# A spectral MLP on one core: the inverse transform as plain fp32 matmuls, and a weight conversion whose last addition is done by a DMA

## Chip, cores and metric

The kernel runs on one core of a Trainium2 chip. The metric is the device time of one execution in microseconds (us). Before the change it is 1207.77 us, the median of 3 runs (1206.66 to 1209.07).

## What is computed

Two batches of 3008 x 256 go through a Fourier layer, and the 6016 resulting tokens through two gated MLPs. Everything is fp32 on the host side; the MLP weights are float64 in memory.

```python
X = np.fft.rfft(x, axis=1)
Yr = Xr @ w_r - Xi @ w_i + b_r
Yi = Xr @ w_i + Xi @ w_r + b_i
# soft threshold at 0.01 of Yr and Yi
y = np.fft.irfft(Yr + 1j * Yi, n=3008, axis=1)
h = y @ w_in1;  y = (h * sigmoid(1.702 * h)) @ w_out1     # 256 -> 2048 -> 256
h = y @ w_in2;  y = (h * sigmoid(h)) @ w_out2
```

## The kernel before

The program has four stages, one after the other on TensorE (PE).

**Forward** (`fold`, `fwd_mm`): sums and differences of the inputs, then matmuls with cosine and sine matrices in plain fp32. One plain fp32 product is two MATMUL instructions in the trace (line 342).

**Mid** (`mid_mm`, `mid_post`, `mid_fold`): twelve units (b, p, j), each the complex product with w_r and w_i, the soft threshold on ACT and DVE, and folds `f` of sum and difference (line 502, four of 256 columns for each unit).

**Inverse** (`inv_mm`, `inv_post`, `inv_out`): sixteen units (q, b, t). Before it, `fsplit` splits each folded tile `f` into a high part `fh` (an ACT cast to fp32r, line 99) and a low part `fl` (a subtraction, line 100), 24 times. The matrices lie in memory as high and low parts too, and `product` adds up three fp32r matmuls for each product (line 345): high by high, high by low, low by high. The pool `m` has four buffers; each takes the two parts of one matrix, so four of the eight matrices are loaded ahead and four during the inverse, by DMAs that POOL issues (line 125). `inv_post` copies (ACT, line 586) or adds (DVE, lines 607 and 608) the result, and `inv_out` writes the four combinations to `yt` (lines 625 and 629), each of the two halves `mm` apart.

**MLP** (`group`, `out_mm`): two layers l, six blocks i of 1024 tokens (the last of 896), eight groups p in a block. A group has 21 matmuls into `x` (line 737) and 24 out of the gated `g` into `o` (line 709), of 512 columns in fp32r; the 24 lag by one group. The low part of `g` is a subtraction on POOL or DVE (line 747). `y1` and `y3`, `y2` are summed on DVE at lines 758, 782 and 779.

Beside these stages the float64 weights are converted, a pair at a time. `cv_load` loads a pair, `cv_bits` rebuilds an fp32 value from the bits with one ACT and five DVE instructions (lines 163 to 172), as two parts `a` and `c`; `settle` adds them (line 225, on POOL or DVE); `window` then places the pair (`place_in`, `place_out`: high and low parts, ACT casts and POOL subtractions). One such step is a tick. A pair that has no room yet is spilled to DRAM (line 228) and fetched again later (line 256). `WEIGHTS` sets the order and whether a pair is kept; `CFG` holds the steps at which ticks are made (`tf` forward, `tm` mid, `ti` inverse, `kb` and `kr` the groups of the first and of the later blocks of layer 0), and which engine does each copy of an operation (`V` DVE, `P` POOL). Before the change the out-pairs 0 to 4 of layer 0 are spilled in the mid stage and fetched in the groups p = 0 to 4 of the first block, and the pool `wib` for in-pairs 4 to 7 opens after the first group, when the pool `fs` of the `fh` tiles is closed. In layer 0's later blocks the ticks convert layer 1's weights, all spilled.

Inside a region named in `CFG` with `all`, every engine keeps the order of the program text; elsewhere a scheduler orders the engines that are not named. `hook(h)` in `group` puts the ticks' parts between a group's matmuls: `window` at 1 or 3, loading at 4, `settle` at 6.

Of the kernel before, what the change touches and what calls it, by code (L numbers as in the profile page):

```python
# [56 lines left out]
def spectral_mlp_kernel(ctx, tc, xin, mfwd, minv, wc, bias, w_in1, w_out1, w_in2, w_out2, outT):  # L57
# [419 lines left out]
    def mid_post(i, ps):  # L477
# [35 lines left out]
    fs = {}  # L513
    fsu = [(q, b, p, j) for q in range(2) for b in range(B) for p in range(2) for j in range(NJ)]
    n_fs = [0]

    def fsplit(k):
        for _ in range(k):
            if n_fs[0] < len(fsu):
                u = fsu[n_fs[0]]  # L520
                f = ft.pop(u)
                hi = fs_p.tile([P, 2 * D], F32R, tag="fh", name="fh")
                lo = slot(0, F32R, "fl")
                split(hi, lo, f, lo_eng=E('fsl', n_fs[0]))
                fs[u] = (hi, lo)
                n_fs[0] += 1
# [25 lines left out]
    def inv_mm(q, b, t):  # L552
# [61 lines left out]
    def inv_out():  # L614
        q, b, ac, rt = ydone.pop(0)
        for mm in range(2):
            col = b * S + (0 if q == 0 else HALF)
            for k in range(4):
                e = E('ivf', (b * 2 + mm) * 4 + k)
                op = e.tensor_sub if k in (0, 3) else e.tensor_add  # L620
                x = ac if k < 2 else rt
                u, v = (row(x, mm, t, 378) for t in range(2))
                if q == 0 and k == 1:
                    y = yt[:, mm, col : col + 376].rearrange("p (g c) -> p g c", g=2)
                    op(y, *(z.rearrange("p (g c) -> p g c", g=2)[:, :, :188] for z in (u, v)))
                    col += 376
                    continue
                for i0, i1 in ((0, 188), (189, 376)) if q == 0 and k == 3 else ((0, 377 if (q, k) == (0, 0) else 376),):
# [346 lines left out]
def _matrices():
    fwd = np.zeros((2, 2, 2, P, NJ * 380), np.float32)
    inv = np.zeros((2, 2, 2, P, MW), np.float32)
    for kind, q, p, cs in np.ndindex(2, 2, 2, 2):
# [13 lines left out]
        else:  # L992
            inv[p, q, cs, :, : 2 * nb * w] = np.stack(_hilo(m), 1).reshape(P, -1)
# [37 lines left out]
```

## Time and profile before

| what | value |
|---|---|
| median of 3 runs | 1207.77 us |
| the profiled execution | 1207.06 us |
| its span, first to last instruction | 1204.9 us |
| busy time PE / ACT / DVE / POOL | 1172.0 / 751.8 / 669.5 / 524.5 us |
| share of PE in the chain that ended last | 76% |
| mean granted TensorE clock | 0.994 |
| moved by DMA | 54.44 MB |

Busy time is the time in which an engine has an instruction under way. The chain that ended last is followed back from the last instruction, at each step to what released it. The granted clock is a share of full speed, 2.4 GHz.

### The profile page before, as it was taken

Reading aid. Unit: us, or ns where it says so; the run is one execution under the profiler, and the core shown is the slowest. Engines: PE = TensorE matmul, PEld = TensorE weight load, DVE = VectorE, ACT = ScalarE, POOL = GpSimd, SP = SyncE. Lnnn points to the kernel's source line nnn. Section 1 sums busy time; section 2 is a strip of 40 time slices with the busy share of each in tenths; the row PEclk is TensorE's granted clock in tenths of the full one; section 3 lists DMA queues with packets and bytes.
Section 4 is the critical chain, followed back from the end, with each engine's and each line's share of the span. In section 5 each row is a group of like instructions: output and inputs, shape, how many; then the busy total and the mean of one; then the engine's idle time right before and its main releaser. Section 6 shows DMA issues by size and latency. Waiting matters only on the chain.

```text
span 1204.9 us, 14433 instructions
## 1 busy us (share of the span) xinstructions
PE 1172.0 (97%) x5044; PEld 936.6 (78%) x5044; DVE 669.5 (56%) x1001; ACT 751.8 (62%) x1422; POOL 524.5 (44%) x429
## 2 busy tenths in 40 slices
PE   7999989799999999999999999999999999999998
PEld 4744489577887887887888978878888888888897
DVE  7868999777557556557465372352442533523422
ACT  2533433577767667667667776676676766766765
POOL 2443343564445444444455755433333333333333
PEclk9999999899999999999999999999999999999999
DMA  7542122021011010110110100000000000000000
GB/s 276 186 151 87 44 88 77 27 70 36 27 43 37 27 52 27 45 53 27 36 50 21 54 27 27 1 36 1 1 35 1 1 35 1 35 1 1 35 1 31
DMA packets 27274, 54.44 MB, mean 45 GB/s; under 512 B 2369, under 2 KB 11585, under 8 KB 26434
## 3 DMA queue, kind: packets, MB, share of 16 engines
q1 hardware_dynamic: 26018, 45.03, 11.1%
q0 software_dynamic: 1184, 8.50, 2.0%
q8 instruction: 39, 0.64, 0.2%
q14 instruction: 33, 0.27, 0.1%
HBM read 41.85 MB, written 11.67 MB: 44 GB/s over the span
## 4 chain that ended last, share of the span: by engine, by line
PE 76%; DVE 10%; ACT 8%; issue 4%; DMA 1%; POOL 0%; SPq 0%; DVEq 0%; ACTq 0%; POOLq 0%
PE o L709 33%; PE x L737 30%; PE psm L470 7%; PE psf L342 4%; ACT yt L740 3%; PE psi L345 2%; ACT g L742 2%; DVE yt L758 1%; DMA raw<-in_x 1%; DVE yt L779 1%; ACT yt L756 1%; DVE x L660 1%; DVE yt L629 1%; ACT x L657 1%; DVE cv_a L170 1%
## 5 line engine op out<-in xcount | busy, mean ns | idle before, releaser
L747 POOL TENSOR_TENSOR g<-yt,g 128x512 fp32r<-128x512 f32 (+1 forms) x282 | 366.9, 1314 | 516.0 <-PE x L737 355.6
L709 PE MATMUL o<-g,wo 128*128 128x512 f32 (+1 forms) x2304 | 562.1, 386 | 4.0 <-POOL wo L100 4.0
L737 PE MATMUL x<-x,wi 128*128 128x512 f32 (+1 forms) x2016 | 505.3, 389 | 12.1 <-DVE yt L758 4.2
L709 PEld LDWEIGHTS o<-g,wo 128*128 128x128 f32 x2304 | 432.7, 188 | 87.5 <-POOL wo L100 5.7
L737 PEld LDWEIGHTS x<-x,wi 128*128 128x128 f32 x2016 | 377.1, 189 | 95.5 <-DVE yt L779 6.3
L740 ACT ACTIVATE yt<-yt 128x512 f32<-128x512 f32 (+1 forms) x288 | 179.2, 622 | 267.1 <-DVE yt L779 216.4
L742 ACT CAST g<-yt 128x512 fp32r<-128x512 f32 (+1 forms) x384 | 234.2, 612 | 11.8
L779 DVE TENSOR_TENSOR yt<-yt,x 128x512 f32<-128x512 f32 (+1 forms) x96 | 64.7, 674 | 213.3 <-PE x L737 212.9
L758 DVE TENSOR_TENSOR yt<-yt,x 128x512 f32<-128x512 f32 (+1 forms) x96 | 64.8, 675 | 163.2 <-ACT yt L756 160.6
L747 DVE TENSOR_TENSOR g<-yt,g 128x512 fp32r<-128x512 f32 (+1 forms) x102 | 71.2, 698 | 76.4 <-ACT g L742 75.5
L470 PE MATMUL psm<-wc_s,xt 128*128 128x512 f32 x192 | 84.5, 592 | 0.0
L470 PEld LDWEIGHTS psm<-wc_s,xt 128*128 128x128 f32 x192 | 36.5, 190 | 43.3 <-issue 41.1
L342 PE MATMUL psf<-m,xf 128*128 128x376 f32 (+2 forms) x208 | 59.2, 447 | 7.7 <-DVE xf L301 7.7
L660 DVE TENSOR_TENSOR x<-yt,x 128x512 fp32r<-128x512 f32 (+1 forms) x48 | 46.4, 968 | 34.2 <-ACT x L657 34.2
L782 DVE TENSOR_TENSOR yt<-yt,x 128x512 f32<-128x512 f32 (+1 forms) x96 | 64.7, 674 | 0.0
L342 PEld LDWEIGHTS psf<-m,xf 128*128 128x128 f32 x208 | 38.3, 195 | 28.0 <-DVE xf L301 9.2
L740 ACT ACTIVATE yt<-x 128x512 f32<-128x512 f32 (+1 forms) x96 | 56.1, 585 | 1.7 <-PE x L737 1.7
L773 ACT COPY yt<-x 128x512 f32<-128x512 f32 (+1 forms) x96 | 55.8, 581 | 1.3 <-PE x L737 1.3
L756 ACT COPY yt<-x 128x512 f32<-128x512 f32 (+1 forms) x96 | 54.9, 572 | 1.7 <-PE x L737 1.7
L771 ACT COPY yt<-x 128x512 f32<-128x512 f32 (+1 forms) x96 | 55.0, 573 | 0.0
L345 PE MATMUL psi<-m,fh 128*128 128x376 f32 (+3 forms) x208 | 49.3, 326 | 3.6 <-DVE rt L608 2.8
L225 POOL TENSOR_TENSOR cv_a<-cv_a,cv_c 128x512 f32<-128x512 f32 x26 | 37.8, 1453 | 14.6 <-DVE cv_c L172 10.6
(90 smaller groups left out, 799.1 us busy)
## 6 DMA issues: line engine op xcount, KB each, us to landing
raw<-in_wi SPq DMA_DIRECT2D x32, 256.0 KB, 3.1
raw<-in_wo SPq DMA_DIRECT2D x16, 512.0 KB, 3.6
raw<-in_x SPq DMA_DIRECT2D x12, 512.0 KB, 4.9
out_t<-yt SPq DMA_DIRECT2D x20, 256.0 KB, 2.0
m<-in_mi POOLq DMA_DIRECT2D x4, 1128.0 KB, 6.0
w_out<-cv_a SPq DMA_DIRECT2D x13, 256.0 KB, 2.0
cv_ld<-w_out SPq DMA_DIRECT2D x13, 256.0 KB, 2.6
m<-in_mi POOLq DMA_DIRECT2D x2, 1134.0 KB, 5.4
```

The lines of the kernel that those rows point to most:

```text
L342: nc.tensor.matmul(ps, hi[:, c : c + P], m[:, k, :w], start=i == 0, stop=i == last)
L345: nc.tensor.matmul(ps, a, z, start=i == 0 and x == 0, stop=i == last and x == 2)
L470: nc.tensor.matmul(t, x[xi][:, mm], wc_s[:, mm, off : off + 2 * D], start=(n == 0), stop=(n == 3 and grp == 1))
L709: nc.tensor.matmul(acc[h, mm], st, mv, start=first and k == 0, stop=last and k == 2)
L737: nc.tensor.matmul(ps, st, mv, start=first and m == 0, stop=m == 2, skip_group_check=True)
L740: nc.scalar.activation(g, g if src is None else src, func)
L742: nc.scalar.copy(gh, g)
L747: eng.tensor_sub(gl, g, r32(gh))
L756: nc.scalar.copy(y1, X)
L758: nc.vector.tensor_add(y1, y1, Y)
L779: nc.vector.tensor_add(y2, y2, X)
L782: nc.vector.tensor_add(y3, y3, Z)
```

## The change

1. The inverse uses plain fp32 products on the folded tiles as they are. `fsplit`, its tiles `fh` and `fl` and the pool `fs` go. The eight matrices are stored once, not as two parts; two share one buffer of pool `m`, so all eight are loaded ahead, by SP.
2. `mid_post` takes the difference of the second half the other way round, so that `mid_fold` is one addition and one subtraction of 512 columns in place of four of 256. `inv_out` handles both halves `mm` in one instruction.
3. All sixteen pairs of layer 0 are kept. The in-pairs 4 and 5 have a pool of their own (`wib0`) from the mid stage on. The mid stage has three ticks, the inverse four, which convert the out-pairs 0 to 3. Fetches of layer 0's out-pairs are gone.
4. In `settle` the addition of the two parts is a DMA that accumulates, issued by POOL, for all 32 pairs.

```diff
-... 'thf': 'PVPVVPVV', 'fsl': 'VPVVVVPV', 'ivf': 'PVVPVVVVVPPVPPVV', ... 'tm': [1, 2, 4, 5, 7, 8], 'ti': [5], ...
+... 'thf': 'VVVP', 'ivf': 'VVVPVVVV', ... 'tm': [2, 6, 10], 'ti': [1, 4, 7, 10], ...
-WEIGHTS = [("in", 0, p, True) for p in range(4)] + [("out", 0, p, False) for p in range(4)]
-WEIGHTS += [("out", 0, 4, False)] + [("in", 0, p, True) for p in range(4, 8)] + [("out", 0, p, True) for p in range(5, 8)]
+WEIGHTS = [("in", 0, p, True) for p in range(6)] + [("out", 0, p, True) for p in range(4)]
+WEIGHTS += [(kind, 0, p, True) for kind, p in (("out", 4), ("in", 6), ("out", 5), ("in", 7), ("out", 6), ("out", 7))]
...
-        m = m_p.tile([P, MW], F32R, tag="m", name="m")[:, : 2 * nb * w]
-        nc.gpsimd.dma_start(out=m, in_=minv[t // 2, q, t % 2][:, : 2 * nb * w])
-        m_tiles[key] = m.rearrange("p (h j c) -> p h j c", h=2, j=nb)
+        m = m_p.tile([P, MW], F32, tag="m", name="m")
+        for cs in range(2):
+            mc = m[:, cs * MW // 2 : cs * MW // 2 + nb * w]
+            nc.sync.dma_start(out=mc, in_=minv[t // 2, q, cs][:, : nb * w])
+            m_tiles[kind, q, t + cs] = mc.rearrange("p (j c) -> p j c", j=nb)
...
-            (nc.vector if wib_p and u[3] else E('cva', u[2])).tensor_add(a, a, c)
+            nc.gpsimd.dma_start(out=a, in_=c, accum_op=ALU.add)
...
-        nc.vector.tensor_sub(sd[:, 1], us, ps[1])
+        nc.vector.tensor_sub(sd[:, 1, :D], us[:, :D], ps[1][:, :D])
+        nc.vector.tensor_sub(sd[:, 1, D:], ps[1][:, D:], us[:, D:])
...
-            for cs in range(2):
-                c = slice(cs * D, (cs + 1) * D)
-                e = E('thf', 4 * i + 2 * q + cs)
-                (e.tensor_add if q == cs else e.tensor_sub)(f[:, c], th[:, 0, c], th[:, 1, c])
+            e = E('thf', 2 * i + q)
+            (e.tensor_sub if q else e.tensor_add)(f, th[:, 0], th[:, 1])
...
-        tiles = [fs[q, b, p, j] for j in range(NJ)]
+        tiles = [(ft[q, b, p, j], None) for j in range(NJ)]
...
-                op(yt[:, mm, col : col + i1 - i0], u[:, i0:i1], v[:, i0:i1])
+                op(yt[:, :, col : col + i1 - i0], u[:, :, i0:i1], v[:, :, i0:i1])
...
-    for p in range(5):
-        moves.setdefault((0, 0, p), []).append(("out", 0, p))
```

The instructions on PE at the start of the inverse; `fh`, `fl` are the parts of a folded tile, `f_` with a number the tile itself. Before:

```order
L470 MATMUL psm<-wc_s,xt_119 128x512 x2
L345 MATMUL psi<-m,fh 128x378 x2
L345 MATMUL psi<-m,fl 128x378
L345 MATMUL psi<-m,fh 128x378 x2
L345 MATMUL psi<-m,fl 128x378
```

and with the change:

```order
L472 MATMUL psm<-wc_s,xt_119 128x512 x2
L344 MATMUL psi<-m,f_703 128x378
L344 MATMUL psi<-m,f_751 128x378
L344 MATMUL psi<-m,f_777 128x378
L344 MATMUL psi<-m,f_703 128x378
```

Three fp32r matmuls have become one plain product, which the hardware trace counts as two instructions.

DVE at the end of the inverse, up to the first `y1` sum of the MLP (line 758 before, 735 now), on which the first group's matmuls wait. Before:

```order
L607 TENSOR_TENSOR ac<-rt,psi 128x376
L660 TENSOR_TENSOR x<-yt,x 128x512
L608 TENSOR_TENSOR rt<-rt,psi 128x376
L629 TENSOR_TENSOR yt<-ac 128x376
L607 TENSOR_TENSOR ac<-rt,psi 128x376
L660 TENSOR_TENSOR x<-tmp,x 128x512
L629 TENSOR_TENSOR yt<-rt 128x376
L608 TENSOR_TENSOR rt<-rt,psi 128x376
L758 TENSOR_TENSOR yt<-yt,x 128x512
```

and with the change:

```order
L590 TENSOR_TENSOR ac<-rt,psi 128x376
L591 TENSOR_TENSOR rt<-rt,psi 128x376
L590 TENSOR_TENSOR ac<-rt,psi 128x376
L591 TENSOR_TENSOR rt<-rt,psi 128x376
L611 TENSOR_TENSOR yt<-ac 128x2x376 x2
L611 TENSOR_TENSOR yt<-rt 128x2x376
L735 TENSOR_TENSOR yt<-yt,x 128x512
```

The splits of the next block's input (`x`) have moved ahead of the last unit, and three outputs of twice the width stand before the sum.

POOL in the first block's groups p = 0 to 2: `wo` and `wi` are the low parts of out- and in-pairs, `g` that of the gated product, `cv_ld` a fetched pair. Before:

```order
L747 TENSOR_TENSOR g<-yt,g 128x512 x3
L100 TENSOR_TENSOR wi_1795<-tmp,wi_1795 128x512
L100 TENSOR_TENSOR wi_1795<-cv_a,wi_1795 128x384
L100 TENSOR_TENSOR wo<-cv_ld,wo 128x512
L747 TENSOR_TENSOR g<-yt,g 128x512 x2
L100 TENSOR_TENSOR wi_1900<-tmp,wi_1900 128x512
L100 TENSOR_TENSOR wi_1900<-cv_a,wi_1900 128x384
L100 TENSOR_TENSOR wo<-cv_ld,wo 128x512
```

and with the change:

```order
L724 TENSOR_TENSOR g<-yt,g 128x512 x3
L100 TENSOR_TENSOR wo<-cv_a,wo 128x512
L724 TENSOR_TENSOR g<-yt,g 128x512 x2
L227 DMA cv_a<-cv_c 128x512
L100 TENSOR_TENSOR wo<-cv_a,wo 128x512
L724 TENSOR_TENSOR g<-yt,g 128x512 x2
L227 DMA cv_a<-cv_c 128x512
L100 TENSOR_TENSOR wi_1648<-tmp,wi_1648 128x512
L100 TENSOR_TENSOR wi_1648<-cv_a,wi_1648 128x384
```

The fetched pairs are gone from the groups, one placement stands in each, and the accumulating DMA stands at a group's end, where DVE did the addition in this block before.

## Rows read from the trace of the kernel before

**Rows 1.** The page: busy time of PE, and the chain that ended last, by engine.

```profile
PE 1172.0 (97%) x5044; PEld 936.6 (78%) x5044; DVE 669.5 (56%) x1001; ACT 751.8 (62%) x1422; POOL 524.5 (44%) x429
...
PE 76%; DVE 10%; ACT 8%; issue 4%; DMA 1%; POOL 0%; SPq 0%; DVEq 0%; ACTq 0%; POOLq 0%
```

**Rows 2.** Windows: the mid stage; columns as in its second line.

```profile
core 0: us, PE busy (x) PEld busy (x) DVE busy (x) ACT busy (x) POOL busy (x), PEclk, DMA share, GB/s
...
67.00:152.00 85.00, 85.00 (x205) 38.63 (x204) 69.22 (x113) 30.87 (x56) 32.24 (x30) 1.00 0.21 69
```

**Rows 3.** Windows: the inverse, then the first block up to its group p = 7.

```profile
151.52:207.91 56.39, 51.12 (x315) 49.67 (x313) 51.76 (x80) 20.00 (x41) 23.15 (x23) 0.97 0.25 88
207.91:288.85 80.94, 71.67 (x290) 55.91 (x289) 64.49 (x102) 53.51 (x98) 42.34 (x31) 0.94 0.14 43
```

**Rows 4.** Waits of PE's weight loads, 151 to 300 us: total, times, longest.

```profile
PEld o L709 <- POOL wo L100: 5.7, 4, 2.4
PEld x L737 <- DVE yt L758: 4.6, 1, 4.6
...
PEld x L737 <- DVE yt L779: 2.1, 2, 1.1
```

**Rows 5.** Windows: plain fp32 products of the forward stage, 24 of 376 columns, then 32 of 190.

```profile
46.47:54.04 7.57, 7.57 (x25) 4.55 (x25) 4.45 (x11) 2.19 (x8) 4.49 (x3) 1.00 0.42 125
54.04:59.21 5.17, 5.17 (x34) 5.16 (x33) 5.01 (x4) 4.63 (x19) 5.04 (x6) 1.00 0.71 245
```

**Rows 6.** Groups of lines: the addition of a pair's two parts, on POOL and on DVE.

```profile
L225 POOL TENSOR_TENSOR cv_a<-cv_a,cv_c 128x512 f32<-128x512 f32 x26 | 37.8, 1453 | 14.6 <-DVE cv_c L172 10.6 <-issue 4.0
...
L225 DVE TENSOR_TENSOR cv_a<-cv_a,cv_c 128x512 f32<-128x512 f32 x6 | 7.3, 1223 | 0.0
```

**Rows 7.** Timeline of DVE, 202 to 217 us: start, length, instruction.

```profile
202.43 1.28 DVE L660 TENSOR_TENSOR x<-yt,x 128x512 fp32r<-128x512 f32 x2
...
214.47 1.32 DVE L629 TENSOR_TENSOR yt<-rt 128x376 f32<-128x376 f32 x1
...
216.16 0.68 DVE L758 TENSOR_TENSOR yt<-yt,x 128x512 f32<-128x512 f32 x1
```

**Rows 8.** Windows: two stretches of the first block, after its first and third idle time.

```profile
216.00:222.00 6.00, 4.75 (x10) 3.31 (x11) 3.33 (x7) 3.30 (x6) 1.90 (x2) 0.50 0.00 0
...
228.40:248.00 19.60, 17.46 (x69) 13.33 (x68) 14.34 (x25) 13.08 (x25) 11.21 (x9) 0.91 0.23 68
```

**Rows 9.** Windows: two groups of a later block, p = 5 and p = 6.

```profile
437.41:447.61 10.20, 10.20 (x47) 8.45 (x46) 6.56 (x9) 6.81 (x13) 4.03 (x4) 1.00 0.16 51
447.61:459.44 11.83, 11.38 (x51) 8.98 (x49) 8.78 (x11) 6.82 (x13) 5.94 (x5) 1.00 0.20 68
```

**Rows 10.** Timeline of DVE in that group p = 6.

```profile
449.21 1.66 DVE L648 TENSOR_TENSOR yt<-yt 128x512 f32<-128x512 f32 x1
450.79 1.51 DVE L168 TENSOR_SCALAR cv_c<-cv_c 128x512 f32<-128x512 f32 x1
452.33 0.43 DVE L169 TENSOR_SCALAR cv_c<-cv_c 128x512 uint32<-128x512 uint32 x1
```

**Rows 11.** Timelines of POOL and of PE in that group.

```profile
448.58 1.74 POOL L225 TENSOR_TENSOR cv_a<-cv_a,cv_c 128x512 f32<-128x512 f32 x1
450.28 1.74 POOL L747 TENSOR_TENSOR g<-yt,g 128x512 fp32r<-128x512 f32 x1
...
455.33 1.89 PE L737 MATMUL x<-x,wi 128*128 128x512 f32 x7 [0.45 <-DVE yt L779]
```

**Rows 12.** DMA issues: KB each, median us from issue to landing.

```profile
w_out<-cv_a SPq DMA_DIRECT2D x13, 256.0 KB, 2.0
...
m<-in_mi POOLq DMA_DIRECT2D x2, 760.0 KB, 7.2
...
bias_hl<-bias_lo POOLq DMA_DIRECT2D x1, 2.0 KB, 5.3
```

**Rows 13.** Line 325, the one DMA from SBUF to SBUF that POOL issues: min/median/max.

```profile
L325 POOL DMA_DIRECT2D bias_hl<-bias_lo x1: 499/499/499, 60.1 to 60.1; - x1
```

More of the change, by code (lines that the diff above doesn't have):

```diff
@@ L10 @@
 F32 = mybir.dt.float32
-CFG = {'lv0': 'V', 'lv': 'VVVVVPVVVVVP', 'dd0': 'VPVVPPPPPVVP', 'dd': 'VVVVVVVVVVPV', 'ths': 'VVVVPV', 'thf': 'PVPVVPVV', 'fsl': 'VPVVVVPV', 'ivf': 'PVVPVVVVVPPVPPVV', 'cva': 'P', 'pol': 'PPPP', 'pil': 'P', 'mvl': 'PVVP', 'xl': 'V', 'xse': 'V', 'gl': 'VPPPPPPP', 'tf': [6, 9, 12], 'tm': [1, 2, 4, 5, 7, 8], 'ti': [5], 'kb': [0, 1, 1, 1, 1, 1, 1, 0], 'kr': [0, 1, 0, 1, 0, 1, 1, 0], 'fa': 3, 'xp': [2, 4, 4, 5], 'xq': [1, 4, 1], 'xs': 4, 'xi': [11, 12, 13, 15], 'xsi': 9, 'ca': 4, 'tl': True, 'fwd': 'Pool,SP', 'rest0': 'all', 'rest1': 'all', 'last1': 'all', 'inv': 'PE', 'mid': 'SP', 'last0': 'all', 'thm': 'A', 'gl0': 'PVPVVVPV', 'gl2': 'PPPPPPPP', 'gl3': 'PPPPPPPV', 'xl0': 'V', 'xl1': 'V', 'pre': 17, 'pre2': 0, 'yd': 6, 'lvb': 6, 'mlp': 'none', 'pr': 'VVVP', 'pf': 'PV', 'eo': '0000', 'ddb': 6, 'mlp1': 'all', 'mlp2': 'all', 'fm': [6, 7, 8, 9, 10, 11], 'f1': 2, 'fsb': 8}
+CFG = {'lv0': 'V', 'lv': 'VVVVVPVVVVVP', 'dd0': 'VPVVPPPPPVVP', 'dd': 'VVVVVVVVVVPV', 'ths': 'VVVVPV', 'thf': 'VVVP', 'ivf': 'VVVPVVVV', 'cva': 'P', 'pol': 'PPPP', 'pil': 'P', 'mvl': 'PVVP', 'xl': 'V', 'xse': 'V', 'gl': 'VPPPPPPP', 'tf': [6, 9, 12], 'tm': [2, 6, 10], 'ti': [1, 4, 7, 10], 'kb': [0, 1, 1, 1, 1, 1, 1, 0], 'kr': [0, 1, 0, 1, 0, 1, 1, 0], 'fa': 3, 'xp': [2, 4, 4, 5], 'xq': [1, 4, 1], 'xs': 4, 'xi': [11, 12, 13, 15], 'xsi': 9, 'ca': 4, 'tl': True, 'fwd': 'Pool,SP', 'rest0': 'all', 'rest1': 'all', 'last1': 'all', 'inv': 'PE', 'mid': 'SP', 'last0': 'all', 'thm': 'A', 'gl0': 'PVPVVVPV', 'gl2': 'PPPPPPPP', 'gl3': 'PPPPPPPV', 'xl0': 'V', 'xl1': 'V', 'pre': 17, 'pre2': 0, 'yd': 6, 'lvb': 6, 'mlp': 'none', 'pr': 'VVVP', 'pf': 'PV', 'eo': '0000', 'ddb': 6, 'mlp1': 'all', 'mlp2': 'all'}
 NUM = dict(tf=[5, 9, 13], tm=[1, 3, 5, 7, 9, 11], ti=[0, 2, 4, 6, 8, 10, 12, 14, 14, 15, 15], kb=[2] * 8, kr=1, fa=3, fe=2, pm=0, nf=4, lvb=6, ddb=8, ivb=1, eob=2, fsb=6, f1=3, f2=0, fm=[7, 8, 9], fi=[1, 1, 2, 2], pre=13, pre2=1, yd=3, psh=0, ie=[12], xp=[1, 3, 4, 5], xq=[1, 2, 2], xs=5, nw=4, xi=[14, 14, 15, 15], xsi=13, rw=2, ca=4, cc=2, tb=1, tmn=1)
@@ L108, in spectral_mlp_kernel @@
     m_tiles = {}
-    m_order = [(kind, q, t) for kind in "fi" for q in range(2) for t in range(4)]
+    m_order = [("f", q, t) for q in range(2) for t in range(4)] + [("i", q, t) for q in range(2) for t in (0, 2)]
     def load_m():
@@ L207, in place_in @@
         )
-    wib_p = []
+    wib_b = []
     spare = []
@@ L454, in spectral_mlp_kernel @@
     region('mid')
-    fs_p = opened("fs", "left", N('fsb'))
+    wib_a = opened("wib0", "left", 2)
     mid_p = opened("mid", "right", 2)
@@ L511, in mid_fold @@
                 ft[q, b, p, -1] = ft.pop((q, b, p, 0))
[L513 to L526, printed above, removed]
     fwd_evac(*prev)
@@ L615, in inv_out @@
         q, b, ac, rt = ydone.pop(0)
[L616 to L628, printed above, removed]
-                    op(yt[:, mm, col : col + i1 - i0], u[:, i0:i1], v[:, i0:i1])
-                    col += i1 - i0
+        col = b * S + (0 if q == 0 else HALF)
+        for k in range(4):
+            e = E('ivf', b * 4 + k)
+            op = e.tensor_sub if k in (0, 3) else e.tensor_add
+            x = ac if k < 2 else rt
+            u, v = (x[:, t * RW : (t + 1) * RW].rearrange("p (m c) -> p m c", m=2) for t in range(2))
+            if q == 0 and k == 1:
+                y = yt[:, :, col : col + 376].rearrange("p m (g c) -> p m g c", g=2)
+                op(y, *(z.rearrange("p m (g c) -> p m g c", g=2)[:, :, :, :188] for z in (u, v)))
+                col += 376
+                continue
+            for i0, i1 in ((0, 188), (189, 376)) if q == 0 and k == 3 else ((0, 377 if (q, k) == (0, 0) else 376),):
+                op(yt[:, :, col : col + i1 - i0], u[:, :, i0:i1], v[:, :, i0:i1])
+                col += i1 - i0
     TB = 1024
@@ L876, in spectral_mlp_kernel @@
                 inv_out()
-            closed("iv", "fs")
-            wib_p.append(opened("wib", "left", NPR // 2))
+            closed("iv")
+            wib_b.append(opened("wib1", "left", 2))
         if N('pre2') and (l, i, p) == (0, last, NPR - 1):
@@ L992, in _matrices @@
         else:
[L993 removed]
+            inv[p, q, cs, :, : nb * w] = m.reshape(P, -1)
     return fwd, inv
```

20 lines of the change are left out of this document (3 added, 17 removed).

## The prediction

> **What bounds the kernel now.** I read the page first: PE is busy 97% of the span, and 76% of the chain that ended last is PE's own work [rows 1]. So a change gains where it takes matmul time or idle PE time away; work of DVE, ACT and POOL counts only where PE waits for it. The windows by stage then say where PE idles. In the mid stage it is busy 85.00 of 85 us [rows 2], so ticks and folds there cost nothing as long as the results come in time. In the inverse 5.3 of 56.39 us are idle, and in the first MLP block 9.3 of 80.94 us [rows 3]. In a later block a group takes 10.20 us, but p = 6 takes 11.83 [rows 9]. Last I read whom PE waits for: in the first block for POOL's `wo` subtraction (5.7 us, four times), for DVE's line 758 (4.6) and line 779 (2.1) [rows 4]. Behind such idle times the granted clock falls: after PE had idled for the 4.6 us it is 0.50 of full speed, its lower level of 1.2 GHz, for 6 us, and it averages 0.91 from 228.4 to 248 us, a stretch that holds one of the `wo` waits [rows 8].
>
> **The sum is made against the profiled execution**, 1207.06 us (span 1204.9 and 2.16 around it), 0.06% under the median of 1207.77.
>
> **Inverse, matmuls: -0.6 us.** The code gives 104 products: twelve units with 2 x 3 of 376 to 378 columns, four with 2 x 4 of 188 to 190. Before, each was three fp32r matmuls; now each is two instructions of a plain fp32 product, the form of the forward stage. There 24 instructions of 376 columns took 7.57 us without idle time, 0.315 each, and 32 of 190 took 5.17, 0.162 each [rows 5]. So 144 x 0.315 + 64 x 0.162 = 55.8 us, against 56.39 now [rows 3]. The matmul work itself grows: PE was busy 51.1 us, partly at a lower clock. The gain exists only if the 5.3 us of idle time go. I take that they do. DVE is busy 51.76 of those 56.39 us, and it loses most of 24 splits, while it gets three ticks more and wider but fewer outputs. The last fold is needed by the seventh of the sixteen units: six units before it, four of 12 x 0.315 and two of 16 x 0.162, are 20.3 us, which is late enough. If the idle time stays, the term is 55.8 + 5.3 - 56.4 = +4.7.
>
> **Start of the MLP: -6.1 us.** The first sum, line 758, stood behind outputs and splits on DVE that were stretched by POOL's outputs: one output of 376 columns took 1.32 us, while two 512-column splits took 1.28 together [rows 7]. PE ran out of work and waited 4.6, and 1.1 of the 2.1 at line 779 soon after [rows 4]. Now no split stands there and POOL has one output left; three outputs of 752 columns remain after the last addition, by 0.64 x 752/512 = 0.94 each 2.8 us. The last addition comes some 1.9 us after the inverse's last matmul, so the sum is ready after 4.7 to 5 us, and PE has 21 matmuls of 10.20/45 = 0.227 us to do without it [rows 9], 4.8 us. I keep 2.0 of the 5.7 us for gates that follow late, so -3.7. With the idle time the 1.2 GHz stretch goes: 4.75 busy us at 0.50 are 2.4 lost [rows 8], so -2.4. The bounds are 0 and -8.1.
>
> **Fetches of out-pairs: -6.7 us.** In the first block each fetched pair was placed in the group before the one that used it, and PE waited 5.7 us for POOL's part [rows 4]. Now `out` pairs are placed two groups or more ahead of their use. I take -5.1, nine tenths of the waits, and for the lowered clock behind the first 17.46 x 0.09 = -1.6 [rows 8]. The ACT cast and POOL subtraction of each fetch go too, and the spills and fetches on SP; none of that was on the chain otherwise.
>
> **Accumulating DMA, first block: +2 us.** No row shows such a DMA. What lies behind it: `settle` issues it at a group's end, and the ACT cast of the placement at hook 3 of the next group waits for it, with that group's gates queued behind on ACT. Between lie 18 matmuls, 18 x 0.227 = 4.1 us. POOL's issue of its only SBUF-to-SBUF DMA took 0.50 us [rows 13], less than the addition of 1.45 on POOL or 1.22 on DVE that goes [rows 6]. The landing is bounded by 2.0 us (the same 256 KB from the same tile, by SP) and 7.2 (the slowest that POOL issued, 760 KB); the one DMA from SBUF to SBUF by POOL took 5.3 for 2 KB in a busy stretch [rows 12]. At 2.0 the cost is 0, at 7.2 it is 6 ticks x 3.1 = 18.6 us. I go by the row with the same size and tile, with as much again and a little for the adding, 4.4, and charge 2 us for six ticks. The Trainium skill, "DMA: Bandwidth & Descriptors", Anatomy of one DMA, fits 2.0 us plus bytes at 436 GB/s for a DMA issued by POOL: an estimate of 2.6 us here, by which this term would be 0. It does not say what accumulating adds, and no run here shows it yet.
>
> **Later blocks of layer 0: -5.2 us.** In group p = 6 the additions of `xsums` and the five DVE instructions of a tick meet POOL's addition: while L225 ran for 1.74 us on POOL, L648 took 1.66, and L168, which met the POOL instruction after it, 1.51 [rows 10, 11]. A 512-column addition took 0.64 undisturbed [rows 7], and the next instruction of L168's kind 0.43 [rows 10], so DVE came to line 779 some 2.1 us late, and PE idled 0.45 there [rows 11]; the group is 1.63 us longer than p = 5 [rows 9]. With the addition gone from POOL, `g` is subtracted a little earlier and meets one DVE instruction, not three. I take 1.3 of the 1.63 for each of the four blocks; the bounds are 0 and 6.5.
>
> **Costs at nothing.** The mid stage's folds and the halved difference (covered by PE, [rows 2]; uncovered, a fold of 512 columns costs about 0.64); the DMA's reads and writes in the forward and mid stages, where DVE and ACT wait for them with buffers of several units in hand; the loads of the matrices, now on SP, half the bytes and all before the inverse; the spills behind the accumulation on SP, for which only the next layer waits.
>
> **Sum:** -0.6 - 6.1 - 6.7 + 2 - 5.2 = -16.6, so 1207.06 - 16.6 = **1190.5 us**. Measurement tells about 0.2%, 2.4 us, from no change.
>
> **Rivals.**
> (a) *Half of it.* Either the inverse keeps its idle time (+5.3 against my sum: 1195.8), or the later groups p = 6 stay long since `g` still meets DVE (+5.2: 1195.7), or the start of the MLP is as late as before, with the table load and the gates ACT's to do first (+6.1: 1196.6). For it: DVE is still busy for most of the inverse, and one buffer `rt` ties ACT to DVE there. Two of the three give about 1202. Against it: each wait named above is for an instruction that the change removes or moves.
> (b) *Slower, by late landings.* If the accumulating DMA takes long (it reads, adds and writes, and other loads share the DMA engines), ACT stands at hook 3 in each of the first block's six ticks, and PE soon after. With the landing L the cost is 6 x (L - 4.1). My sum without the +2 is -18.6, so the point is L = 7.2 us, just the slowest POOL row [rows 12]. At L = 10 the cost is 35.4, and the time 1207.06 - 18.6 + 35.4 = 1223.9. Against it: the row of this size is at 2.0.
> (c) *Nothing.* The change removes waits whose place others take: +4.7 in the inverse, 0 at the start, -6.7 + 2 for fetches and new waits, 0 in the later blocks: 1207.06 + 0, about 1207. For it: the plain products alone are more matmul work than before, and DVE's outputs still stand before line 758.
>
> **How the numbers follow.** My sum 0.62, (a) 0.25, (b) 0.07, (c) 0.06. The time is that of the sum, 1190.5. The range must leave out 0.2: it leaves out (b), (c) and the ends of the others, and runs from 1184 (the lower bounds of the start and of the accumulating DMA, which together take 4 off, and of the later blocks, 1.3, and about 1 more from the short waits) to 1202.5 (two of the failures in (a)). Faster by over 0.2% means under 1205.4: the sum and (a) whole, 0.87. Within 0.2%: part of (c), 0.04. Slower: (b) and the rest, 0.09.
>
> **What would show it.** Right: line 345's plain products start 0.315 us apart with no idle time and the inverse stays near 56 us; PE's first wait in the MLP is under 2 us and the clock stays at 1.00 there; no wait on `wo` is left; group p = 6 takes 10.5 us or less; the DMA of line 225 lands in 2 to 5 us. Wrong: ACT or DVE waiting on that DMA with PE idle behind them; matmuls of the inverse waiting for `rt`; line 779 still late in p = 6.

## The result, and the profile after

The changed kernel takes **1191.64 us** (median of 4 runs, 1190.61 to 1192.25) against 1207.29 for the kernel before (4 runs). The ratio is 0.9863, with a 95% interval of 0.9851 to 0.9874. The profiled execution took 1191.14 us and its span is 1189.4; the forecast was 1190.5.

The page of the changed kernel: busy time by engine, the granted clock in 40 slices, and the chain that ended last, to be read against [rows 1].

```profile
PE 1170.6 (98%) x4940; PEld 923.2 (78%) x4940; DVE 628.5 (53%) x969; ACT 740.8 (62%) x1398; POOL 480.3 (40%) x399
...
PEclk9999999999999999999999999999999999999999
...
PE 71%; ACT 5%; DVE 2%; issue 2%; DMA 0%; POOL 0%; DVEq 0%; ACTq 0%; POOLq 0%
```

PE is busy only 1.4 us less, while the span is 15.5 us shorter: most of what went was idle time. DVE's share of the chain fell from 10% to 2%.

The windows of the changed kernel: mid stage, inverse, and the first block up to nearly the same matmul as in [rows 3]; columns as there.

```profile
67.00:152.00 85.00, 85.00 (x205) 38.67 (x204) 63.27 (x117) 31.38 (x60) 26.32 (x20) 1.00 0.29 85
152.12:207.67 55.55, 55.55 (x210) 37.45 (x208) 43.84 (x66) 14.17 (x29) 13.26 (x9) 1.00 0.12 29
207.67:278.00 70.33, 67.58 (x289) 53.20 (x288) 48.16 (x79) 48.86 (x87) 30.31 (x26) 1.00 0.23 57
```

The inverse has no idle time: PE is busy 55.55 of 55.55 us, where it was 51.12 of 56.39 [rows 3]. PE now has more work there, and DVE less, 43.84 us for 51.76. The first block up to p = 7 takes 70.33 us for 80.94; PE's idle time fell from 9.3 to 2.8 us, and the clock is at 1.00.

The waits of PE's weight loads in the changed kernel, 151 to 300 us (total, times, longest), against [rows 4]:

```profile
PEld o L686 <- POOL g L724: 1.8, 2, 1.2
PEld o L686 <- ACT g L719: 1.8, 2, 1.4
PEld x L714 <- ACT yt L733: 1.5, 2, 1.0
...
PEld x L714 <- DVE yt L756: 0.5, 2, 0.4
```

The wait on `wo` (5.7 us, four times) and the one on the first `y1` sum (4.6) are gone. DVE's timeline at the start of the MLP shows why, against [rows 7]:

```profile
209.27 1.79 DVE L611 TENSOR_TENSOR yt<-ac 128x752 f32<-128x752 f32 x2
210.97 0.93 DVE L611 TENSOR_TENSOR yt<-rt 128x752 f32<-128x752 f32 x1
211.83 0.68 DVE L735 TENSOR_TENSOR yt<-yt,x 128x512 f32<-128x512 f32 x1
```

Three outputs stand before the sum, 0.90 to 0.93 us each, and the sum starts 4.16 us after the MLP's first matmul (207.67); before it was 8.25 (207.91 to 216.16).

The accumulating DMA is line 227 now. What the trace says of that line: length of the issue on POOL (ns, min/median/max), who waited for it, and the time to landing.

```profile
L227 POOL DMA_DIRECT2D cv_a<-cv_c x32: 848/866/1002, 42.1 to 611.5; - x32
...
  ACT wi L99: 8.1, 5
  ACT wo L99: 7.2, 4
  DVE tmp L202: 4.8, 4
...
DMA to landing us min/median/max: 3.2/3.3/7.9
```

It lands in 3.3 us at the median. The 7.9 falls in the forward stage, where other loads are under way too. ACT waits for it at the placements, 15.3 us in nine casts of the whole run: it comes to a cast earlier than the 4.1 us behind the issue that the forecast worked out from PE's matmuls. Once in the first block this reaches PE. ACT stands for 3.28 us at a cast, the gates and the copy of line 733 come late behind it, and PE waits 0.57 us:

```profile
236.43 0.62 ACT L99 CAST wo<-cv_a 128x512 fp32r<-128x512 f32 x1 [3.28 <-DMA cv_a<-cv_c]
```

```profile
241.11 0.96 PE L714 MATMUL x<-x,wi 128*128 128x512 f32 x3 [0.57 <-ACT yt L733]
```

The Trainium skill, "DMA: Bandwidth & Descriptors", Anatomy of one DMA (2.0 us plus bytes at 436 GB/s), gives an estimate of 2.6 us, 0.7 too little for the median here.

For the rest of the text the span is cut at places that every kernel here has. "First block" runs from the first `x` matmul of the MLP to the second `y1` sum of the second block, "blocks 1 to 4" from there to the same place in the last block of layer 0. The two rows of the kernel before, then of the changed one (windows, columns as above):

```profile
207.91:314.07 106.16, 96.72 (x397) 75.87 (x396) 80.20 (x124) 75.12 (x137) 53.31 (x40) 0.95 0.12 38
314.07:647.45 333.38, 329.83 (x1440) 268.90 (x1440) 193.50 (x260) 226.50 (x404) 152.30 (x113) 1.00 0.12 39
```

```profile
207.67:303.39 95.72, 92.82 (x398) 73.45 (x396) 63.11 (x100) 70.21 (x126) 42.61 (x36) 1.00 0.20 50
303.39:631.77 328.38, 327.21 (x1440) 269.89 (x1440) 188.05 (x261) 226.64 (x404) 138.98 (x113) 1.00 0.19 53
```

All kernels, from their profiled executions (us):

| kernel | mid | inverse | first block | blocks 1 to 4 | behind them | span |
|---|---|---|---|---|---|---|
| before | 84.73 | 56.39 | 106.16 | 333.38 | 557.48 | 1204.9 |
| changed | 85.20 | 55.55 | 95.72 | 328.38 | 557.60 | 1189.4 |
| e1_engine_add | 85.16 | 55.55 | 98.30 | 333.41 | 557.33 | 1196.7 |
| e3_old_ticks | 85.20 | 55.55 | 101.47 | 328.32 | 559.50 | 1196.8 |
| e8_inverse_only | 85.19 | 55.55 | 101.03 | 333.38 | 558.67 | 1200.8 |
| e2_before_dma | 84.72 | 59.15 | 106.20 | 328.34 | 558.73 | 1204.1 |
| e9_dma_without_mid_spills | 84.74 | 60.64 | 106.17 | 328.35 | 557.47 | 1204.0 |
| e12_dve_add | 85.16 | 55.55 | 98.18 | 328.40 | 557.34 | 1191.9 |
| e4_bounce | 85.12 | 55.55 | 124.88 | 328.68 | 558.16 | 1221.1 |
| e5_kr_shift | 85.12 | 55.55 | 95.79 | 326.82 | 557.57 | 1189.2 |
| e6_preload | 85.12 | 55.55 | 94.70 | 328.32 | 558.38 | 1189.4 |
| e10_both | 85.16 | 55.55 | 94.88 | 326.83 | 557.62 | 1186.8 |
| e11_fifth_tick | 85.20 | 55.55 | 96.03 | 326.80 | 557.59 | 1188.8 |

What is missing to the span lies ahead of the mid stage, 66.6 to 68.7 us, and varies with the first loads from run to run. So the columns say what an edit did to a stage, the ratios what it did to the time. A column comes from one execution of each kernel; where an edit does not reach a stage, columns mostly agree within 0.1 us (the inverse is 55.55 in all ten kernels that have the new one). The last column is 1.1 to 1.9 us longer than the changed kernel's in e2, e3 and e8, though none of their edits stands there. The ratios of e5, e6 and e11 can't be told from the changed kernel's; for these three the columns decide. The 15.56 us of the span are 0.84 in the inverse, 10.44 in the first block and 5.00 in blocks 1 to 4, less 0.7 elsewhere.

### The profile page after: what moved, and what is told of

The parts are those of the page before. It is cut to its first block, busy times and chain, and to the rows that moved or that the text cites. A ratio compares the mean times of both kernels' runs of the same rounds, so it can differ in the third digit from the quotient of the medians.

```text
span 1189.4 us, 14160 instructions
## 1 busy us (share of the span) xinstructions
PE 1170.6 (98%) x4940; PEld 923.2 (78%) x4940; DVE 628.5 (53%) x969; ACT 740.8 (62%) x1398; POOL 480.3 (40%) x399
## 4 chain that ended last, share of the span: by engine, by line
PE 71%; ACT 5%; DVE 2%; issue 2%; DMA 0%; POOL 0%; DVEq 0%; ACTq 0%; POOLq 0%
PE o L686 38%; PE x L714 33%; ACT yt L717 2%; ACT g L719 1%; ACT x L637 1%; ACT yt L733 1%; DVE x L640 0%; DVE yt L735 0%; DVE yt L756 0%; DVE yt L690 0%; ACT yt L750 0%; DMA cv_a<-cv_c 0%; ACT yt L748 0%; ACT yt L690 0%; ACT wi L99 0%
## 5 line engine op out<-in xcount | busy, mean ns | idle before, releaser
L724 POOL TENSOR_TENSOR g<-yt,g 128x512 fp32r<-128x512 f32 (+1 forms) x282 | 361.0, 1293 | 537.7 <-PE x L714 357.7
L640 DVE TENSOR_TENSOR x<-yt,x 128x512 fp32r<-128x512 f32 (+1 forms) x48 | 49.9, 1041 | 35.9 <-ACT x L637 35.9
L750 ACT COPY yt<-x 128x512 f32<-128x512 f32 (+1 forms) x96 | 55.8, 581 | 0.8 <-PE x L714 0.8
L344 PE MATMUL psi<-m,f 128*128 128x376 f32 (+3 forms) x192 | 54.7, 440 | 0.0
L344 PEld LDWEIGHTS psi<-m,f 128*128 128x128 f32 x192 | 35.3, 190 | 18.5 <-issue 0.5
```

Source lines behind the costliest of these rows:

```text
L344: nc.tensor.matmul(ps, hi[:, c : c + P], m[:, k, :w], start=i == 0, stop=i == last)
L724: eng.tensor_sub(gl, g, r32(gh))
L750: nc.scalar.copy(y3, X)
```

## The experiments

The kernel before was timed again beside each set of runs: 1208.49 us for the first four, 1208.58 for e4, e5 and e6, 1209.05 for the last four.

**e1: the changed kernel with the addition on the engines again.**

```diff
-            nc.gpsimd.dma_start(out=a, in_=c, accum_op=ALU.add)
+            (nc.vector if wib_b and u[3] else E('cva', u[2])).tensor_add(a, a, c)
```

> The changed kernel with the addition of a pair's two parts back on POOL and DVE, as before. My account: POOL's addition is what makes group p = 6 of layer 0's later blocks long, so the four blocks take about 83.4 us again in place of 82.1, together +5.0 us, and the first block changes by 0 to +2 (DVE gets its six additions of 1.2 us back, ACT no longer waits for a landing): 1197 to 1199 us. Rival: the later blocks became shorter through something else (pairs kept, fewer spills), then they stay at 82.1 and the time at 1191 to 1193 us.

Measured: 1198.84 us, ratio to before 0.9917 [0.9905, 0.993]. Blocks 1 to 4 lose 5.03 us, as the account of p = 6 has it. The first block loses 2.6 where the DMA was thought to cost 2: with it gone the block is longer, not shorter. The waits of PE's weight loads in this kernel, 150 to 300 us:

```profile
PEld x L714 <- DVE yt L756: 3.5, 5, 1.6
```

That wait is 0.5 us in the changed kernel. The window of the first block:

```profile
207.63:305.93 98.30, 93.56 (x398) 72.99 (x396) 70.53 (x106) 70.06 (x126) 39.56 (x30) 1.00 0.11 33
```

In the first block DVE does the additions when no DMA does them, six of 0.68 us, 4.1 in all, ahead of the sums on which PE waits.

**e3: the changed kernel with the old ticks**: out-pairs 0 to 4 converted in the mid stage, spilled, and fetched in the first block. The inverse and the DMA stay.

```diff
-... 'tm': [2, 6, 10], 'ti': [1, 4, 7, 10], ...
+... 'tm': [1, 2, 4, 5, 7, 8], 'ti': [5], ...
+    for p in range(5):
+        moves.setdefault((0, 0, p), []).append(("out", 0, p))
```

(`WEIGHTS` is the old one, too.)

> The changed kernel with the ticks and the order of the weights of before: out-pairs 0 to 4 spilled in the mid stage and fetched in the first block's groups. My account: the waits of PE for POOL's wo subtraction are those of the fetched pairs and come back, with the lowered clock behind the first: +5 to +7 us, 1196.5 to 1198.5 us, all of it in the first block. Rival: those waits came from the backlog of DVE and POOL after the splits of the inverse; then without the splits fetched pairs are placed in time, and the time is within 2 us of the changed kernel's 1191.6.

Measured: 1198.31 us, 0.9911 [0.9897, 0.9925]; the first block is 5.75 us longer than in the changed kernel. Its waits in the same stretch:

```profile
PEld o L686 <- POOL wo L100: 6.9, 4, 2.3
```

The wait on the fetched pairs is back, four times, as in [rows 4]. The window of the first block, whose mean clock is 0.98 here:

```profile
207.53:309.00 101.47, 94.81 (x398) 74.53 (x396) 64.99 (x107) 73.15 (x132) 50.63 (x42) 0.98 0.22 55
```

**e8: the part of the inverse alone**, e1's and e3's edits together: plain products, resident matrices, new folds and outputs.

> Only the plain fp32 inverse with its resident matrices, wider folds and outputs; ticks and order of weights as before, additions on POOL and DVE as before. My account, if the parts add up: the inverse gives 0.8 and the start of the MLP some 3 to 6 us against before, the later blocks nothing (83.4 each) and the waits on wo stay: 1201 to 1204 us. Rival: the parts need each other, since the plain inverse alone is 4 us more of matmul work whose cover (DVE's free time) is only used by the moved ticks: 1206 us or more.

Measured: 1202.38 us, 0.9947 [0.9935, 0.9958]. The window of its first block:

```profile
207.71:308.74 101.03, 93.72 (x398) 73.23 (x396) 74.82 (x113) 72.94 (x132) 47.64 (x36) 1.00 0.13 40
```

The first block is 5.13 us shorter than before: 3.0 of PE's busy time, since the clock stays up, and 2.1 of idle time. The wait on `wo` is still there, 6.7 us. Blocks 1 to 4 are what they were.

With before, e8, e1, e3 and the changed kernel the first block can be taken apart, and the parts do **not** add up. The DMA changes it by +0.44 with the old ticks (e3 less e8) and by -2.58 with the new ones. The new ticks change it by -2.73 with the engines adding (e1 less e8) and by -5.75 with the DMA. In idle time of PE alone the DMA is worth 0.65 us with the old ticks (7.31 to 6.66) and 1.84 with the new ones (4.74 to 2.90): while PE waits for the fetched pairs, most of what DVE's additions cost is hidden, and once the fetches go, DVE's sum at line 756 ends last. The other part of the difference is PE's busy time, 1.09 us longer with the old ticks and 0.74 shorter with the new ones. Of the four kernels only e3 shows a clock under 1.00 in this block, although e8 has the same waits on `wo`; how much of that part is the DMA's doing is not shown. In e2 below, the DMA alone in the kernel before is worth nothing in this block either.

**e2: the kernel before with the DMA alone.**

```diff
-            (nc.vector if wib_p and u[3] else E('cva', u[2])).tensor_add(a, a, c)
+            nc.gpsimd.dma_start(out=a, in_=c, accum_op=ALU.add)
```

> The kernel before with the accumulating DMA alone. My account: the later blocks of layer 0 take 82.1 in place of 83.4 us, -5.0 together, and the first block loses or gains at most 2: 1200 to 1204 us. Rival: where fetched pairs and ticks are placed in the same group, the landing of 3.3 us holds ACT up and the first block pays over 5 us: 1207 us or more.

Measured: 1207.27 us, 0.999 [0.998, 1.0]. Blocks 1 to 4 gain their 5.04 us and the first block nothing, and then the inverse is 2.76 longer. The time is in the rival's range, but the place was expected by neither theory. The window of its inverse:

```profile
151.72:210.87 59.15, 52.15 (x315) 49.63 (x313) 54.20 (x84) 20.41 (x42) 24.82 (x24) 0.97 0.23 84
```

PE's idle time there is 7.0 us, for 5.3 in [rows 3]; DVE, the tight engine, is busy 54.20 us. The waits of SP's queue up to 215 us name a suspect:

```profile
SPq L228 <- DMA cv_a<-cv_c: 24.8, 5, 6.1
```

The spill on SP now stands until the DMA has landed, 24.8 us in five waits, where it stood 5.5 us for POOL's addition before, and the next loads are queued behind it.

**e9: the same, but the five pairs that the mid stage spills are added by the engine.**

```diff
-            nc.gpsimd.dma_start(out=a, in_=c, accum_op=ALU.add)
+            if u[3] or u[1]:
+                nc.gpsimd.dma_start(out=a, in_=c, accum_op=ALU.add)
+            else:
+                E('cva', u[2]).tensor_add(a, a, c)
```

> The kernel before with the accumulating DMA for all pairs but the five that the mid stage spills, which POOL adds as before. In the run with the DMA for all pairs, SP's spill waited 24.8 us for five landings (5.5 us for POOL's additions before), and the raw loads behind it on SP came late. If that is what lengthened the inverse from 56.4 to 59.2 us, it is 56 to 57 us here, the later blocks still take 82.1, and the time is 1202 to 1204.5 us. Rival: the kept pairs' placements wait for the landing on ACT and DVE; then the inverse stays near 59 us and the time at 1206 to 1208.

Measured: 1206.96 us, 0.9981 [0.9972, 0.9991]. The inverse takes 60.64 us, longer still, so the theory of the held queue **falls**. The waits of SP's queue in this kernel up to 215 us (line 231 is the spill here):

```profile
SPq L231 <- POOL cv_a L228: 5.6, 5, 2.4
```

SP's wait at the spill is back at 5.6 us, and the loss stays. So the DMA of the kept pairs that are converted ahead of the mid stage is enough for it.

The traces show where the loss begins. The last load of the forward stage, line 151, lands 6.2 us after its issue at 64.1 us in the kernel before, and 13.0 us after its issue at 62.3 in e9 (10.5 in e2); POOL's loads of the matrices and, in e2 and e9, the accumulating DMAs are under way beside it. Before, then e9:

```profile
DMA to landing us min/median/max: 6.2/6.2/6.2
```

```profile
DMA to landing us min/median/max: 13.0/13.0/13.0
```

So DVE converts this pair late (line 168 starts at 76.0 us in e9 and 74.4 in e2, for 71.0 before), the mid stage's first tick is late (line 154 issues its first load at 78.9 and 77.3, for 75.1), and so is its last (line 172 starts at 135.0 and 133.7, for 131.1). From there on DVE has the same order in all three kernels, and in the inverse PE waits for the mid stage's last differences on DVE, which it did not before:

```profile
PE psi L348 <- DVE sd L486: 3.4, 2, 2.6
```

In e2 this wait is 1.7 us (line 483). The last tick is late by 3.9 and 2.6 us, the inverse longer by 4.25 and 2.76. Which of the loads beside it delays the load of line 151 was not tested, and the traces are of one execution each. In the changed kernel's inverse the DMA costs nothing, whether with its three ticks in the mid stage (55.55 us, as without the DMA in e1) or with the old six (e3, as without in e8).

**e4: late landings on purpose.** In the first block each sum is written to DRAM and read back before the placement may use it.

```diff
             nc.gpsimd.dma_start(out=a, in_=c, accum_op=ALU.add)
+            if u[3] and wib_b:
+                d = dram_p.tile([P, 2 * CU], F32, name=f"h_{u[0]}{u[1]}_{u[2]}")
+                nc.sync.dma_start(out=d, in_=a)
+                nc.sync.dma_start(out=a, in_=d)
```

> The changed kernel, with the six pairs that the first block converts sent to DRAM and back by SP after the accumulation, so that they are ready about 3.3 + 2.0 + 2.7 = 8.0 us after the accumulation is issued, and POOL issues nothing more. The prediction's formula: 6 x (8.0 - 4.1) = 23 us more, 1215 us. Rival: ACT's free time in a group and the lag of the second matmuls take up most of it, PE waits under 1.5 us per tick: at most 9 us more, 1192 to 1200 us.

Measured: 1219.44 us, 1.0096 [1.0075, 1.0117], and the first block is 29.2 us longer than in the changed kernel, where 23 were expected. The four casts of out-pairs start 8.1 to 10.2 us after POOL's issue, 9.5 in the mean. The forecast's formula, 6 x (L - 4.1), gives 32 for that. The window of the block:

```profile
209.40:334.28 124.88, 102.38 (x396) 79.15 (x395) 63.03 (x100) 70.08 (x126) 42.43 (x36) 0.92 0.23 64
```

Of the 29.2 us, 19.6 are idle time of PE (22.5 us for 2.9) and 9.6 longer busy time, at a mean clock of 0.92. The formula speaks of idle time only; for that it gives too much, and that it comes near the whole is chance, since it leaves the clock out. The waits of PE's weight loads up to 300 us, then those of ACT in the block (lines are four further on here):

```profile
PEld x L718 <- ACT yt L737: 11.5, 2, 7.1
PEld x L718 <- DVE yt L760: 5.9, 3, 3.0
```

```profile
ACT wo L99 <- DMA cv_a<-h_out: 28.6, 4, 9.5
```

So the way in which rival (b) would have worked is real: ACT stands at the cast, its copies for the next group queue behind it, and PE runs dry. What the rival lacked was a slow landing.

**e12: the addition on DVE throughout the MLP, no DMA.**

```diff
-            nc.gpsimd.dma_start(out=a, in_=c, accum_op=ALU.add)
+            (nc.vector if wib_b else E('cva', u[2])).tensor_add(a, a, c)
```

> The changed kernel with the addition of the two parts on DVE in all of the MLP (the later blocks' too), and as in the kernel before ahead of it. If it is the meeting of POOL's addition with DVE's two-input instructions that makes p = 6 long, the DVE addition of 0.6 us alone costs less than POOL's: the four later blocks take 82.1 to 82.8, 1 to 3 us less together than with POOL's addition, and the time is 1195.5 to 1198. Rival: any addition of an engine lies on the path to the sum at line 756; then the blocks stay at 83.4 and the time at 1198 to 1199.

Measured: 1194.26 us, 0.9883 [0.9867, 0.9898]. The window of blocks 1 to 4:

```profile
306.19:634.59 328.40, 327.20 (x1440) 270.04 (x1440) 197.29 (x277) 226.68 (x404) 126.18 (x97) 1.00 0.12 40
```

That is the 328.38 of the DMA and 5.0 us less than with POOL's addition, where 1 to 3 were expected, although DVE is busy 9.2 us longer. So in the later blocks the loss was not the addition but that POOL did it beside DVE, and DVE could do it for nothing. What the DMA has over it is the first block alone, 98.18 for 95.72.

**e5: the last tick of a later block moved from p = 6 to p = 4.**

```diff
-... 'kr': [0, 1, 0, 1, 0, 1, 1, 0], ...
+... 'kr': [0, 1, 0, 1, 1, 1, 0, 0], ...
```

> The changed kernel with the ticks of layer 0's later blocks at p = 1, 3, 4, 5 in place of 1, 3, 5, 6. If what is left of the long group p = 6 (10.87 us against 10.20) is the meeting of a tick with the preparation of the next block's input on DVE, the four blocks lose 0.5 us each: -2.0, 1189.6 us. Rival: the tick's cost moves with it, since two or three ticks in a row fill DVE and ACT as well: within 0.5 us of 1191.6.

Measured: 1190.18 us, 0.9851 [0.9836, 0.9865]; blocks 1 to 4 are 1.56 us shorter than in the changed kernel, for 2.0 expected. The starts of the `y1` sums bound p = 6 and p = 7; DVE's timeline of the changed kernel, then of e5:

```profile
435.72 0.69 DVE L735 TENSOR_TENSOR yt<-yt,x 128x512 f32<-128x512 f32 x1 [2.06 <-ACT yt L733]
...
446.59 0.69 DVE L735 TENSOR_TENSOR yt<-yt,x 128x512 f32<-128x512 f32 x1 [2.06 <-ACT yt L733]
...
456.90 0.67 DVE L735 TENSOR_TENSOR yt<-yt,x 128x512 f32<-128x512 f32 x1
```

```profile
436.64 0.69 DVE L735 TENSOR_TENSOR yt<-yt,x 128x512 f32<-128x512 f32 x1 [2.05 <-ACT yt L733]
446.84 0.69 DVE L735 TENSOR_TENSOR yt<-yt,x 128x512 f32<-128x512 f32 x1 [2.05 <-ACT yt L733]
457.27 0.68 DVE L735 TENSOR_TENSOR yt<-yt,x 128x512 f32<-128x512 f32 x1
```

In the changed kernel p = 6 takes 10.87 us (11.83 in [rows 9]) and p = 7 10.31; in e5, without the tick, p = 6 takes 10.20 and p = 7 10.43. The tick at p = 6 had not become free.

**e6: ACT's function table loaded ahead, in the last unit of the inverse.** `pre` is the unit of the inverse with which ACT loads the table for the first gates. The units are 0 to 15, so with 17 it is not loaded ahead.

```diff
-... 'pre': 17, ...
+... 'pre': 15, ...
```

> The changed kernel with ACT's function table for the first activation loaded at the end of the inverse, where ACT is idle for 6.8 us, in place of in front of the first activation (1.28 us). If the first gates are what PE waits for at the start of the MLP (1.4 and 0.6 us), PE waits 1.0 to 1.3 us less: 1190.3 to 1190.6 us. Rival: DVE's outputs in front of the first sum set that start, then within 0.3 us of 1191.6.

Measured: 1190.83 us, 0.9856 [0.9839, 0.9873]; the first block is 1.02 us shorter. In the changed kernel ACT's timeline has the table load ahead of the first gate; in e6 the gate needs none there, and starts 4.87 us after the MLP's first matmul in place of 5.85:

```profile
212.23 1.28 ACT L717 ACT_TABLE_LOAD   x1
213.52 0.63 ACT L717 ACTIVATE yt<-yt 128x512 f32<-128x512 f32 x1
```

```profile
212.89 0.63 ACT L717 ACTIVATE yt<-yt 128x512 f32<-128x512 f32 x1 [0.30 <-DVE yt L735]
```

**e10: e5's and e6's edits together.**

> The changed kernel with both the shifted ticks of the later blocks and the earlier table load. If the two gains add up (1.6 and 1.0 us in the stages they touch): 1189.0 us, ratio to the kernel before 0.984. Rival: one shifts what the other gained: over 1190.

Measured: 1188.57 us, 0.9833 [0.9819, 0.9846]. The first block (94.88) and blocks 1 to 4 (326.83) keep both gains. This version is below the kernel before and, by its ratio, the changed one.

**e11: e10 with a fifth tick in the inverse**, taken from p = 6 of the first block.

```diff
-... 'ti': [1, 4, 7, 10], 'kb': [0, 1, 1, 1, 1, 1, 1, 0], ...
+... 'ti': [1, 4, 7, 10, 13], 'kb': [0, 1, 1, 1, 1, 1, 0, 0], ...
```

> As the last one, with a fifth tick in the inverse, where DVE is idle for 11.7 of 55.6 us, and one fewer in the first block, at its p = 6. If the first block's ticks cost what is left there, it takes 0.5 to 1 us less: 1188.0 to 1188.5. Rival: the tick's placement meets the start of the MLP, which is bound by ACT and DVE: 1189.5 to 1192.

Measured: 1190.5 us, 0.9853 [0.984, 0.9867]; the first block is 1.15 us longer than in e10. The time is in the rival's range. In the waits of PE's weight loads DVE's sum at line 756 is late, where e10 has 1.1 us in three waits for it:

```profile
PEld x L714 <- DVE yt L756: 2.8, 2, 2.3
```

Only a little of it is at the start of the MLP, where the first sum comes 4.50 us after the first matmul, for 4.15 in e10. The longest wait stands further on in the first block, behind its first tick. With one pair more converted in the inverse, that tick has an in-pair, where e10 has an out-pair. An in-pair's placement begins on DVE: DVE stands until the accumulating DMA has landed, the sum comes behind the placement, and PE waits. DVE, then PE:

```profile
235.81 0.29 DVE L202 TENSOR_TENSOR tmp<-cv_a 128x128 f32<-128x128 f32 x1 [0.88 <-DMA cv_a<-cv_c]
...
236.75 0.68 DVE L756 TENSOR_TENSOR yt<-yt,x 128x512 f32<-128x512 f32 x1
```

```profile
237.48 2.37 PE L714 MATMUL x<-x,wi 128*128 128x512 f32 x9 [1.86 <-DVE yt L756]
```

So the edit changed the order of the pairs too, and the loss is rival (b)'s, by way of DVE. The inverse itself keeps its 55.55 us; whether a fifth tick would pay with another order was not tried.

## Why the prediction came out as it did

**Inverse, -0.6: right.** The stage takes 55.55 us for 55.8 worked out from the forward stage's prices [rows 5], and the idle time went whole. Of its gain of 0.84 about half comes back at the border to the mid stage, as said below. Rival (a)'s first case did not occur, and the resident matrices on SP cost nothing there.

**Start of the MLP, -6.1: right.** e8 measures -5.1 for the whole first block, 3.0 of it in busy time and 2.1 in idle time. At the start itself PE's idle time went from 4.55 us in two waits to 1.11 in two, so -3.4 for the 3.7 taken. The sum came earlier than forecast, at 4.16 us; what is left are the gates, with the 1.28 us table load before the first. The busy time is 3.0 us shorter for the 2.4 taken for the clock. What the block gives back lies further on: PE's own waits on `wo` are 1.0 us longer (5.0 for 4.0).

**Fetches of out-pairs, -6.7: right in size only beside the DMA.** Put back, they cost 5.75 us (e3). Without the DMA their removal is worth 2.7 (e8 to e1), since the sum at line 756 then takes their place as the last to end. The 1.6 us for the clock are not shown to be theirs: e3 has 2.0 us more busy time of PE (94.81 for 92.82), but e8, with the fetches and 6.7 us of waits on `wo`, has a clock of 1.00 in the block, and e8 to e1 is 0.2.

**Accumulating DMA in the first block, +2: the step that failed.** It is -2.6 with the new ticks (e1). The landing was 3.3 us and not 4.4. The 4.1 us that the forecast set against it are 18 matmuls of PE, but ACT runs ahead of PE: it comes to the casts of the out-pairs 0.05 to 5.0 us after the issue, stands there up to 3.28 us, and PE waits for that once, 0.57 us. So the cost is small, but not by the forecast's formula, which e4 does not bear out for idle time either. And the text took DVE's six removed additions [rows 6] into no term: it set POOL's issue against them and left it there. They are worth something because the other terms had taken away most of the wait that hid them. POOL's issue, taken as 0.50 us from [rows 13], is 0.87, still less than the 1.45 of its addition.

The errors in these three offset one another: -6.1 - 6.7 + 2 is -10.8, and the first block gained 10.44. That the total came so near, 1191.6 for 1190.5, is in part luck.

**Later blocks, -5.2: right in sum, not in one detail.** Blocks 1 to 4 gain 5.00 us, all of it from the addition leaving POOL (e1, e2, e12). It was to show as a group p = 6 of 10.5 us or less; it is 10.87, and the rest comes from p = 7 (10.31 for 10.69). The window of p = 7 in the kernel before:

```profile
459.44:470.13 10.69, 10.36 (x46) 8.22 (x45) 8.80 (x10) 8.63 (x16) 6.18 (x5) 1.00 0.07 25
```

DVE's timeline of the changed kernel in p = 6, to be read against [rows 10]:

```profile
437.32 0.69 DVE L628 TENSOR_TENSOR yt<-yt 128x512 f32<-128x512 f32 x1
437.93 1.51 DVE L170 TENSOR_SCALAR cv_c<-cv_c 128x512 f32<-128x512 f32 x1
...
441.73 0.68 DVE L756 TENSOR_TENSOR yt<-yt,x 128x512 f32<-128x512 f32 x1
```

and POOL's there:

```profile
436.68 0.86 POOL L227 DMA_DIRECT2D cv_a<-cv_c  x1
437.87 1.29 POOL L724 TENSOR_TENSOR g<-yt,g 128x512 fp32r<-128x512 f32 x1 [0.32 <-ACT g L719]
```

The second sum of `xsums` takes 0.69 us, for 1.66 when POOL added beside it. The tick's first instruction still takes 1.51, since it still meets POOL's subtraction of `g`, as the forecast's "meets one DVE instruction, not three" has it.

**Costs at nothing: right**, but for 0.4 to 0.5 us in the mid stage, which is longer in every kernel with the new inverse and not in e2 and e9. Nearly all of it lies at the border: from the start of the last eight matmuls of the mid stage to the first of the inverse it is 3.43 us for 3.03. Both stages together went from 141.12 to 140.75 us. The DMA in the forward and mid stages is free in the changed kernel, but not in the kernel before, where e2 and e9 pay for it in the inverse.

**Rivals.** (a) fell in all three prices, though `g` does still meet DVE in p = 6, as its second case says. (b) had the right mechanism, as e4 and e11 show, and the wrong landing time. (c) fell; something like it is what the DMA alone does in the old kernel (e2), a gain of 5 us in one stage and most of it given back in others.

## What to carry to other kernels

A term found from one wait holds only while that wait ends last. Ask of each removed instruction whether another term takes its cover away; here the DMA was worth nothing in the first block with the fetches in place, and 2.6 us without them. And an instruction on one engine can lengthen those that run beside it on another (0.69 to 1.66 us for a sum on DVE beside POOL's addition here): before handing it to a DMA, try it on the other engine, which here gave the whole gain of the later blocks.

## What the runs showed of the hardware that was not expected

- An accumulating DMA of 256 KB from SBUF to SBUF lands 3.3 us after its issue by POOL at the median, 3.2 at least. In the forward and mid stages, beside other loads, it took up to 7.9 us in the changed kernel and 13.1 in e9. The issue holds POOL for 0.84 to 1.01 us.
- The last block of layer 0 (448 columns in each matmul) takes two lengths with the same instructions. Over the 81.6 us behind blocks 1 to 4, PE got through 376 matmuls in ten of these kernels and 373 in e3, e4 and e6, about 0.7 us less work. What decides it is not known.
